# Splitting the first block's x loads over two DMA queues by partition halves

## The chip, the cores and the metric

The kernel runs on one core of a Trainium2 chip. The core has five engines that run their own instruction streams: TensorE (PE; its weight loads are shown apart as PEld), VectorE (DVE), ScalarE (ACT), GpSimd (POOL) and SyncE (SP), which only issues transfers and waits. SyncE, ScalarE and GpSimd can each issue DMA transfers on a queue of their own; the core's 16 DMA engines serve all of these queues. The metric is the time of the kernel on the device in microseconds (us); lower is better. Times are medians of several runs. A profile is one execution, with the times of every instruction and every DMA packet.

## What is computed

x is 2048 tokens of 640 features in bf16. Two branches are mixed by a gate for each token: A is linear attention with 32 heads of 20 features and a softmax feature map, B is a gated feed-forward layer of width 1728.

```python
def reference(A_x, A_wqkv, A_w_phi, A_wo, B_x, B_w_gate, B_w_up, B_w_down, gate_w):
    x = A_x
    g = _sigmoid((x * gate_w).sum(-1, keepdims=True))
    a = _A_ref(x, A_wqkv, A_w_phi, A_wo)
    b = _B_ref(x, B_w_gate, B_w_up, B_w_down)
    return g * a + (1 - g) * b

def _A_ref(x, wqkv, w_phi, wo):
    qkv = (x @ wqkv).reshape(B, S, 3, H, Dh).transpose(2, 0, 3, 1, 4)
    q, k, v = qkv[0], qkv[1], qkv[2]
    pq, pk = q @ w_phi, k @ w_phi                       # per head
    phi = lambda p: concat([softmax(p), softmax(-p)])   # for q and for k
    num = phi_q @ (phi_k.T @ v)
    den = phi_q @ phi_k.sum(0) + 1e-6
    return (num / den) @ wo

def _B_ref(x, w_gate, w_up, w_down):
    return (gelu(x @ w_gate) * (x @ w_up)) @ w_down
```

## The kernel before

The 2048 tokens are 16 tiles of 128 rows, in four blocks of four tiles. Every projection needs x with its features on the partitions (`xT`), so x must be transposed. For blocks 2 to 4 this is done by transposing DMA loads (`xturn`, L236). The first block is wanted sooner: its 512 rows are loaded as they are into `xtok` (`x4`, L227: partition p gets rows 4p to 4p+3, so the tiles are interleaved), and PE transposes them (`x_transpose`, L333). Each tile is transposed in 64-row halves, r = 0 for partitions 0 to 63 and r = 1 for 64 to 127, ten small matmuls against an identity matrix for each half. The result in PSUM is copied into `xT` by DVE (L355, tiles 0 and 2), by ACT (L353, tile 1) or by both (L350 and L351, tile 3).

`loads` (L222) gives the opening order of each queue. SyncE: the two x loads (`xload`, L229, tiles 0 and 1, then 2 and 3, 320 KB each), the v part of the attention weights in six pieces (L251, the first 128 rows in two pieces with the keys `("wv", 0)` and `"wv0"`), early up weights (L254), then transposing loads of x and of the k and q weights (L238, L234). ScalarE: an Exp on a constant (L241), ahead of which the compiler puts the load of the table of functions, then two small loads, `w_phi` (L276, which waits for a mask from GpSimd) and the gate row `gz` (L279).

`attention_state` (L684) is PE's order: nine matmuls on constants while nothing has landed (L689), the transposes of tiles 0 and 1, six small matmuls on constants (L696), the transposes of tiles 2 and 3, and then the v projection of the four tiles (`v_step`, L475, matmuls on L480). Its first steps take w piece `("wv", 0)` for tiles 0 and 1, and then `"wv0"`. After it come the gate column (L371), up projections of the first block held for later (`up_ahead`, L557), v for further tiles, and the fold of `w_phi` into the k weights (L406), which reads block-diagonal copies of `w_phi` that DVE makes (L362). The k and q projections, the Gram sums and the feed-forward layer follow, nearly all of it bound to PE.

`_Sched` sets the waits: each operation names keys that it reads and writes, and waits for the events recorded under these keys (L66). A DMA takes its queue's next lane, a semaphore of its own (L84): SyncE has 16 lanes, ScalarE 4. The keys `("xtok", t)` are read by the transposes, and by `up_ahead` (L560) and `before_num` (L857) as guards, since the memory of `xtok` is used again later.

Of the kernel before, what the change touches and what calls it, by code (L numbers as in the profile page):

```python
# [107 lines left out]
class _Kernel:  # L108
# [113 lines left out]
    def loads(self):  # L222
        sc, nc = self.sc, self.nc
# [2 lines left out]

        x4 = self.x[0:self.BT, :].rearrange("(p j) n -> p j n", j=self.TB)  # L227

        def xload(q, j):  # L229
            sc.dma(q, lambda e: e.dma_start(self.xtok[:, j:j + 2, :], x4[:, j:j + 2, :]),  # L230
                   writes=[("xtok", j), ("xtok", j + 1)])

        def wload(T, c0, key):
            sc.dma("sp", lambda e: e.dma_start_transpose(T[:, :, :], self.wqkv[:, c0:c0 + D]), writes=[key])  # L234
# [1 line left out]
        def xturn(t, n):  # L236
            a, z = t * P, (t + n) * P
            sc.dma("sp", lambda e: e.dma_start_transpose(self.xT[:, :, a:z], self.x[a:z, :]),  # L238
                   writes=[("xT", k) for k in range(t, t + n)])
        sc.op("pool", lambda e: e.memset(self.gz[:, :], 0.0), writes=["gz"])  # L240
        sc.op("act", lambda e: e.activation(self.gtmp[:, 0:1], self.nc.const_aps.tensor(1.0, [P, 1], BF16), AF.Exp),  # L241
              writes=["gtmp"])
        sc.op("pool", lambda e: e.memset(self.ident[:, :], 0.0), writes=["ident"])
        sc.op("pool", lambda e: e.affine_select(self.ident[:, :], self.ident[:, :], pattern=[[-1, P]],
                                                compare_op=ALU.not_equal, fill=1.0, base=0, channel_multiplier=1),
              writes=["ident"])
        xload("sp", 0)
        xload("sp", 2)
        for kt in range(KD):
            for a, z, key in ((0, self.VA, ("wv", 0)), (self.VA, D, "wv0")) if kt == 0 else ((0, D, ("wv", kt)),):  # L250
                sc.dma("sp", lambda e: e.dma_start(self.w3[:, kt, a:z], w3[:, kt, 2 * D + a:2 * D + z]), writes=[key])  # L251
        u3 = self.wu.rearrange("(kt p) n -> p kt n", p=P)
        a, z = self.UP[0] * P, 7 * P
# [5 lines left out]
               writes=["wul"])  # L259
# [5 lines left out]
        for i in range(KD):  # L265
# [12 lines left out]
            reads=[("mask", 1)], writes=["wphi"])  # L278
# [54 lines left out]
    def x_transpose(self, t, ek):  # L333

        sc = self.sc
        b, w = (0, 4, 2, 6)[t], self.D // 2
        bks = (b, b + 1)
        pv = self.bank(b, 1024).bitcast(BF16).rearrange("p (r c) -> p r c", r=2)[:, :, 0:w]
        for c in range(self.KD):
            for r in (0, 1):  # L340
                a = 64 * r
                sc.op("pe", lambda e: e.transpose(  # L342
                    pv[:, r, c * 64:(c + 1) * 64], self.xtok[a:a + 64, t, c * P:(c + 1) * P],
                    self.ident[a:a + 64, a:a + 64]),
                    reads=[("xtok", t), "ident"], writes=[("ps", bks[r])], signal=(c == self.KD - 1))
        out = self.xT[:, :, t * P:(t + 1) * P].rearrange("p c (r t) -> p c r t", t=64)
        src = pv.rearrange("p r (c t) -> p c r t", t=64)
        rd = [("ps", b) for b in bks]
        if ek == "ad":
            sc.op("act", lambda e: e.activation(out[:, :, 0, :], src[:, :, 0, :], AF.Copy), reads=rd[:1], writes=[("xh", t)])  # L350
            sc.op("dve", lambda e: e.tensor_copy(out[:, :, 1, :], src[:, :, 1, :]), reads=rd[1:], writes=[("xT", t)])  # L351
        elif ek == "a":
            sc.op("act", lambda e: e.activation(out, src, AF.Copy), reads=rd, writes=[("xT", t)])  # L353
        else:
            sc.op("dve", lambda e: e.tensor_copy(out, src), reads=rd, writes=[("xT", t)])  # L355
# [201 lines left out]
    def up_ahead(self, j, b, ek):  # L557
        c = (self.UP + self.LATE)[j]
        out, wk = self.upheld(c)
        old = ["wkT"] if c in self.LATE else [("xtok", k) for k in range(4)]  # L560
        for kt in range(self.KD):
            self.mm(b, 0, 512, self.wu_sb[:, kt, c * P:(c + 1) * P], self.xT[:, kt, 0:self.BT], kt == 0,
                    kt == self.KD - 1, [("xT", t) for t in range(4)] + [wk])
        if ek == "d":
            self.sc.op("dve", lambda e: e.tensor_copy(out, self.bank(b)), reads=[("ps", b)], writes=[("upf", c)],
                       guard=old)
        else:
            self.sc.op("act", lambda e: e.activation(out, self.bank(b), AF.Copy), reads=[("ps", b)], writes=[("upf", c)],
                       guard=old)
# [284 lines left out]
        return later  # L854

    def before_num(self):
        return ([("upf", c) for c in self.UP + self.LATE] + ["kstage", "qstage"] + [("wref", k, h) for k in (0, 3) for h in (0, self.HM)] + [("wref", k, 0) for k in (1, 2, 4)] + [("xtok", k) for k in range(4)] + ["wkT", "wqT"] + self.oldk)  # L857

    def num(self, t, banks=(0, 6)):
        old = self.before_num()  # L860
# [222 lines left out]
```

## Time and profile before

| | us |
|---|---|
| median of 3 runs | 281.86 |
| lowest and highest | 281.77, 281.93 |
| the profiled execution, own time | 281.68 |
| its span, first to last instruction | 280.4 |
| around the span | 1.28 |

The profile of this execution is read in views: the page with busy shares, the chain of work that ended last, the timeline of an engine, the DMA issues with their time to landing, and windows, which give busy time and DMA rate by stretch. All times in these views are microseconds from the start of the span. A line such as `4.72 0.47 PE ps L342 x20` is: start, duration, engine, what it writes, source line, count. In square brackets stands the idle time before a group and what ended it. The opening in numbers, from the DMA issues and the timelines:

| what | issued on | issue begins | to landing | first use |
|---|---|---|---|---|
| x, tiles 0 and 1, 320 KB | SyncE | 0.80 | 2.9 | 3.76 |
| x, tiles 2 and 3, 320 KB | SyncE | 1.27 | 3.4 | 4.72 |
| w `("wv", 0)`, 64 KB | SyncE | 1.73 | 3.2 | 5.12 |
| w `"wv0"`, 96 KB | SyncE | 2.19 | 3.2 | 5.43 |
| early up weights, 480 KB | SyncE | 4.57 | 4.8 | 10.66 |
| w_phi, 25 KB | ScalarE | 2.86 | 3.8 | 6.64 |

### The profile page before, as it was taken

What the parts mean: (1) busy time and instruction counts of PE and PEld (TensorE: products, weight loads), DVE (VectorE), ACT (ScalarE), POOL (GpSimd) and SP (SyncE); (2) the same over time, 40 slices, a digit from 0 to 9 for tenths busy, and PEclk for the clock granted to TensorE, in tenths of its full rate; (3) what the DMA queues carried; (4) which work ended last, traced back from release to release, by engine and by line L of the source; (5) the groups of instructions that cost most, each with busy time, mean ns of one, the idle gap of its engine ahead of it and who ended that gap; (6) DMA issues with size and microseconds to landing.
All of it is one profiled execution on the core that took longest, in us unless ns stands there. A gap on an engine that the chain in (4) does not pass through costs nothing.

```text
span 280.4 us, 7063 instructions
## 1 busy us (share of the span) xinstructions
PE 276.6 (99%) x2994; PEld 168.1 (60%) x3006; DVE 177.3 (63%) x342; ACT 106.4 (38%) x205; POOL 14.4 (5%) x69
## 2 busy tenths in 40 slices
PE   8999999999999999999999999999999999999997
PEld 4576766666765444444444444445777777777785
DVE  2666999999998524233242234878884883883801
ACT  3347877878783423222323223122112112112021
POOL 7411001101000000000000000000000000000000
DMA  7999069887899910000000000101133142232221
GB/s 217 224 220 189 6 136 165 171 163 146 162 191 273 347 41 0 2 0 0 1 2 0 0 0 2 23 2 26 26 50 108 35 76 56 62 59 66 71 75 47
DMA packets 59994, 24.11 MB, mean 86 GB/s; under 512 B 50874, under 2 KB 59450, under 8 KB 59962
## 3 DMA queue, kind: packets, MB, share of 16 engines
q1 hardware_dynamic: 59296, 23.63, 37.7%
q8 instruction: 23, 0.38, 0.6%
q10 hardware_dynamic: 666, 0.03, 0.2%
q14 instruction: 9, 0.07, 0.1%
HBM read 9.04 MB, written 2.62 MB: 42 GB/s over the span
## 4 chain that ended last, share of the span: by engine, by line
PE 97%; DMA 1%; issue 0%; SPq 0%; ACT 0%
PE ps L466 52%; PE ps L935 29%; PE ps L832 6%; PE ps L610 4%; PE ps L480 2%; PE ps L875 2%; PE ps L646 2%; DMA xtok<-in_A_x_dram 1%; PE ps L406 1%; PE ps L342 0%; SPq L230 0%; ACT outsb L948 0%; PE ps L371 0%
## 5 line engine op out<-in xcount | busy, mean ns | idle before, releaser
L809 ACT ACTIVATE gl<-ps 128x512 bf16<-128x512 f32 x52 | 31.1, 597 | 71.2 <-PE ps L466 56.3
L466 PE MATMUL ps<-xT,wu_sb 128*128 128x512 bf16 x214 | 52.9, 379 | 0.3
L466 PE MATMUL ps<-xT,wg_sb 128*128 128x512 bf16 x214 | 52.7, 379 | 0.3
L466 PE MATMUL ps<-w,xT 128*128 128x368 bf16 (+6 forms) x340 | 51.6, 303 | 0.0
L813 DVE TENSOR_TENSOR hT<-ps,gl 128x512 bf16<-128x512 f32 x34 | 23.4, 691 | 44.5 <-PE ps L466 44.5
L935 PE MATMUL ps<-wd_sb,hT 64*128 64x320 bf16 x648 | 48.2, 296 | 0.0
L948 ACT ACTIVATE outsb<-ps,Gm 128x320 bf16<-128x320 f32 (+2 forms) x31 | 14.6, 516 | 70.3 <-PE ps L935 70.3
L466 PEld LDWEIGHTS ps<-w,xT 128*128 128x128 bf16 x340 | 32.1, 98 | 14.6
L935 PEld LDWEIGHTS ps<-wd_sb,hT 64*128 64x128 bf16 x648 | 30.9, 94 | 11.8
L466 PEld LDWEIGHTS ps<-xT,wu_sb 128*128 128x128 bf16 x220 | 21.5, 98 | 25.6
L466 PEld LDWEIGHTS ps<-xT,wg_sb 128*128 128x128 bf16 x220 | 21.2, 98 | 25.2 <-issue 0.2
L935 PE MATMUL ps<-wo_sb,goT 64*128 64x320 bf16 (+2 forms) x340 | 26.5, 288 | 0.0
L628 DVE TENSOR_REDUCE Dk<-Ek 128x66 f32<-128x1320 bf16 x16 | 24.3, 1520 | 2.3 <-ACT gcol L539 2.3
L637 DVE TENSOR_TENSOR Ek<-Ek,Dk 128x1320 bf16<-128x1320 bf16 x16 | 24.5, 1533 | 0.5
L904 DVE TENSOR_TENSOR O<-ps,RH 128x640 bf16<-128x640 f32 x32 | 24.8, 815 | 0.0
L549 ACT ACTIVATE Ek<-ps 128x627 bf16<-128x627 f32 x32 | 20.5, 693 | 6.0 <-PE ps L610 4.5
L549 ACT ACTIVATE Eqt<-ps 128x627 bf16<-128x627 f32 x32 | 20.6, 704 | 2.4 <-PE ps L466 2.4
L935 PEld LDWEIGHTS ps<-wo_sb,goT 64*128 64x128 bf16 x340 | 15.8, 94 | 5.5
L832 PE MATMUL ps<-xT,wg_sb 64*128 64x512 bf16 x80 | 17.6, 376 | 0.0
L832 PE MATMUL ps<-xT,wu_sb 64*128 64x512 bf16 x80 | 17.6, 376 | 0.0
L935 PE MATMUL ps<-wd_sb,xT 64*128 64x320 bf16 (+2 forms) x270 | 16.0, 269 | 0.0
L893 DVE RECIPROCAL RH<-ps 128x32 f32<-128x32 f32 x16 | 5.7, 356 | 13.4 <-PE ps L875 13.4
(97 smaller groups left out, 222.3 us busy)
## 6 DMA issues: line engine op xcount, KB each, us to landing
out_dram<-outsb SPq DMA_DIRECT2D x7, 320.0 KB, 2.9
wd_sb<-in_B_w_down_dram SPq DMA_DIRECT2D x1, 2080.0 KB, 12.2
wg_sb<-in_B_w_gate_dram SPq DMA_DIRECT2D x5, 224.0 KB, 3.1
wg_sb<-in_B_w_gate_dram SPq DMA_DIRECT2D x5, 192.0 KB, 3.0
wu_sb<-in_B_w_up_dram SPq DMA_DIRECT2D x5, 192.0 KB, 3.9
wo_sb<-in_A_wo_dram SPq DMA_DIRECT2D x1, 800.0 KB, 10.2
xtok<-in_A_x_dram SPq DMA_DIRECT2D x2, 320.0 KB, 3.2
w<-in_A_wqkv_dram SPq DMA_DIRECT2D x4, 160.0 KB, 3.6
```

The lines of the kernel that those rows point to most:

```text
L466: self.sc.op("pe", lambda e: e.matmul(self.ps[:, bank * 512 + c0:bank * 512 + c0 + n], lhs, rhs, start=first, stop=fin), reads=reads, writ ...
L549: self.sc.op("act", lambda e: e.activation(dst, src, AF.Exp, scale=scale), reads=[("ps", b), ("ps", b + 1)], writes=[(name, sl, s)])
L610: self.sc.op("pe", lambda e: e.matmul(out, self.xT[:, kt, t * P:(t + 1) * P], self.w3[:, kt, c:c + 2 * n].rearrange("p (r w) -> p r w", w= ...
L628: self.sc.op("dve", lambda e: e.tensor_reduce(self.Dk[:, se, 0, :].rearrange("p (u h) -> p u h", h=self.HG), self.k_view(se), AX.X, ALU.ad ...
L637: sc.op("dve", lambda e: e.tensor_tensor(v, v, R.rearrange("p (u h) -> p u h", h=self.HG).unsqueeze(3).to_broadcast([P, 2 * self.G, self.H ...
L809: self.sc.op("act", lambda e: e.activation(self.gl[:, slot, :], self.bank(bank), AF.Gelu_apprx_tanh), reads=[("ps", bank)], writes=[("gl", ...
L813: self.sc.op("dve", lambda e: e.tensor_tensor(self.hT(b, c), up, self.gl[:, slot, :], ALU.mult), reads=[upk, ("gl", slot)], writes=[("hT", ...
L832: sc.op("pe", lambda e: e.matmul(self.bank(bk), w[a:a + 64, kt, c * P:(c + 1) * P], self.xT[a:a + 64, kt, b * self.BT:(b + 1) * self.BT], ...
L893: dve(lambda e: e.reciprocal(R(0), Dn[1]), rb, [key(0)], guard=old)
L904: dve(lambda e, o=o, f=f, s=s: e.tensor_tensor(o, V[s][:, :, 0:DH], f, ALU.mult), rb[2 * s:2 * s + 2] + [key(6 + s)], [("O", s, sl)], guar ...
L935: sc.op("pe", lambda e: e.matmul(self.bank(bk, w), lhs, rhs, start=opens and x == 0, stop=end and not opens, skip_group_check=True), reads ...
L948: sc.op("act", lambda e: e.activation(dst, self.bank(bk, w), AF.Copy, scale=g), reads=rd, writes=wr)
```

## The change

Each of the two x loads becomes two loads, one of partitions 0 to 63 on SyncE's queue and one of partitions 64 to 127 on ScalarE's queue. Both are placed ahead of the Exp on L241, so that ScalarE issues its two halves first. The keys get a third part, the half; a transpose of half r waits for the load of half r alone, and the later guards name both halves. Nothing else is edited: the bytes loaded and the matmuls are the same.

```diff
-        def xload(q, j):
-            sc.dma(q, lambda e: e.dma_start(self.xtok[:, j:j + 2, :], x4[:, j:j + 2, :]),
-                   writes=[("xtok", j), ("xtok", j + 1)])
+        def xload(j):
+            for q, r in (("sp", 0), ("act", 1)):
+                a = 64 * r
+                sc.dma(q, lambda e: e.dma_start(self.xtok[a:a + 64, j:j + 2, :], x4[a:a + 64, j:j + 2, :]),
+                       writes=[("xtok", j, r), ("xtok", j + 1, r)])
...
         sc.op("pool", lambda e: e.memset(self.gz[:, :], 0.0), writes=["gz"])
+        xload(0)
+        xload(2)
         sc.op("act", lambda e: e.activation(self.gtmp[:, 0:1], self.nc.const_aps.tensor(1.0, [P, 1], BF16), AF.Exp),
               writes=["gtmp"])
...
-        xload("sp", 0)
-        xload("sp", 2)
...
-                    reads=[("xtok", t), "ident"], writes=[("ps", bks[r])], signal=(c == self.KD - 1))
+                    reads=[("xtok", t, r), "ident"], writes=[("ps", bks[r])], signal=(c == self.KD - 1))
...
-        old = ["wkT"] if c in self.LATE else [("xtok", k) for k in range(4)]
+        old = ["wkT"] if c in self.LATE else [("xtok", k, r) for k in range(4) for r in (0, 1)]
```

The list in `before_num` is changed in the same way.

More of the change, by code (lines that the diff above doesn't have):

```diff
@@ L856, in before_num @@
     def before_num(self):
-        return ([("upf", c) for c in self.UP + self.LATE] + ["kstage", "qstage"] + [("wref", k, h) for k in (0, 3) for h in (0, self.HM)] + [("wref", k, 0) for k in (1, 2, 4)] + [("xtok", k) for k in range(4)] + ["wkT", "wqT"] + self.oldk)
+        return ([("upf", c) for c in self.UP + self.LATE] + ["kstage", "qstage"] + [("wref", k, h) for k in (0, 3) for h in (0, self.HM)] + [("wref", k, 0) for k in (1, 2, 4)] + [("xtok", k, r) for k in range(4) for r in (0, 1)] + ["wkT", "wqT"] + self.oldk)
     def num(self, t, banks=(0, 6)):
```

## The prediction

> **What bounds the kernel now.** I read the busy shares first: TensorE (PE) is busy in 276.6 of 280.4 us. Next the chain of waits, which says what keeps PE from its work. Its columns are start, duration (us) and what ran. Apart from the first 5 us it is PE all the way to the final output, so a shift of the point from which PE is dense goes one to one into the time.
>
> ```profile
> span 280.4 us, 7063 instructions
> PE 276.6 (99%) x2994; PEld 168.1 (60%) x3006; DVE 177.3 (63%) x342; ACT 106.4 (38%) x205; POOL 14.4 (5%) x69
> ...
> 0.80 0.40 SPq L230
> 1.21 0.06 issue
> 1.27 3.41 DMA xtok<-in_A_x_dram
> 4.68 0.05 issue
> 4.72 0.47 PE ps L342 x20
> 5.19 4.56 PE ps L480 x36
> ```
>
> So the second x load (issued at 1.27, landed 4.68) is the one on the chain. But the timeline of the weight loads (PEld) shows a second limit right behind it:
>
> ```profile
> 3.76 0.35 PEld L342 LDWEIGHTS ps<-ident,xtok 64*128 64x128 bf16 x20 [0.15 <-DMA xtok<-in_A_x_dram]
> 4.72 0.35 PEld L342 LDWEIGHTS ps<-ident,xtok 64*128 64x128 bf16 x20 [0.49 <-DMA xtok<-in_A_x_dram]
> 5.12 0.11 PEld L480 LDWEIGHTS ps<-w,xT 128*128 128x128 bf16 x2
> 5.43 2.62 PEld L480 LDWEIGHTS ps<-w,xT 128*128 128x128 bf16 x24 [0.20 <-DMA w<-in_A_wqkv_dram]
> ```
>
> The v projection does its first two steps at 5.12 and 5.24 and then waits till 5.43 for the second w piece, "wv0": 96 KB, issued on SyncE's queue at 2.19, 3.2 us to landing, so 5.39. From 5.43 PE is dense. **That 5.43 is the number to forecast.** Everything later has slack: the DMA view gives the next w piece 2.67 + 3.2 = 5.87 against a first use at 6.33, and the first up weights 4.57 + 4.8 = 9.37 against 10.66.
>
> Third, the windows of the DMA: columns are the window, busy time of each engine, clock share, DMA share and GB/s.
>
> ```profile
> 1.75:2.25 0.50, 0.50 (x3) 0.20 (x2) 0.00 (x0) 0.49 (x2) 0.39 (x3) 1.00 0.79 133
> 2.25:2.75 0.50, 0.50 (x3) 0.15 (x1) 0.00 (x0) 0.04 (x1) 0.36 (x4) 1.00 0.75 251
> 2.75:3.25 0.50, 0.50 (x2) 0.15 (x1) 0.00 (x0) 0.00 (x0) 0.36 (x4) 1.00 1.05 399
> 3.25:3.75 0.50, 0.50 (x4) 0.26 (x2) 0.00 (x0) 0.00 (x0) 0.39 (x3) 1.00 1.02 390
> ```
>
> After a ramp of 1 us, which moves 0.5 x (133 + 251) = 192 KB, the engines are full at some 395 GB/s. The two x loads are 2 x 320 KB = 655 thousand bytes, so 463 of them move in the full stretch, in 463 / 395 = 1.17 us. Bytes, not issue, set when x and the w pieces behind it land.
>
> **The change part by part.**
>
> SyncE's queue: it issues two x loads before and after, with 64 rows in place of 128. Issues take 0.40 (x, 128 rows) and 0.44 to 0.47 each for w pieces and the up weights (the six w issues span 2.80), of few or many rows alike, so I cost a half at 0.40 and leave the w issues at 1.73 and 2.19. What waits behind them on this queue (six w loads, the up weights, the transposing loads) moves by nothing. Were a half's issue cheaper, at most 0.8 would be saved there; but the w bytes would still stand behind the x bytes.
>
> ScalarE's queue, in order, from the timeline of ACT:
>
> ```profile
> 0.80 1.28 ACT L241 ACT_TABLE_LOAD   x1 [0.80 <-PEq L1068]
> 2.09 0.20 ACT L241 ACTIVATE gtmp<-const-bfloat16-1.0 128x1 f32<-128x1 bf16 x1
> 2.86 0.44 ACTq L276 DMA_DIRECT2D wphi_sb<-in_A_w_phi_dram  x1
> 3.33 0.67 ACTq L279 DMA_DIRECT2D gz<-in_gate_w_dram  x1
> 4.37 0.70 ACT L353 ACTIVATE xT<-ps 128x640 bf16<-128x640 bf16 x1 [2.07 <-PE ps L696]
> ```
>
> Two issues of 0.40 with 0.06 between go ahead: table load 1.73 to 3.01, Exp to 3.22, then the w_phi load to 3.69 (its wait for the mask ended by 2.86) and the gate row to 4.38. The copy of x tile 1 (L353) begins at 4.37 today, so ACT loses 0.01: 0.92 us of added issue lie in its idle time, 2.09 to 2.86 less the Exp, and 4.00 to 4.37. The cover is then gone: any further ACT delay puts the second projection step, which reads tile 1, behind by as much. w_phi lands some 0.4 later (6.64 to about 7.04); the block-diagonal products on DVE (L362, 2.64 us) end at 9.68 instead of 9.28, and DVE was idle for 0.56 before the gate column at 9.84; their reader on PE (L406) comes at 16.85. Nothing on the path. The gate row lands before 7.5 and is used at 9.6.
>
> Waits: each tile's transposes wait for two semaphores instead of one. Between 0 and two times the 0.05 that the chain shows at such a wait; 0, as both stand where PE waits for the later one anyway. Queued behind them on PE are the fillers and all projections.
>
> The transfers: x still has 655 thousand bytes, but as four loads of 64 rows. No x load of 64 rows is in the trace; the nearest rows are the two 80 KB loads of down weights (64 rows each), which stand in SyncE's queue between the 2080 KB load and wo's 800 KB. Counting bytes back from the end of the queue (931 thousand after 96.0, of which wo is 819), most of them move from 96.0 on:
>
> ```profile
> 95.50:96.00 0.50, 0.50 (x4) 0.24 (x3) 0.00 (x0) 0.50 (x1) 0.00 (x0) 1.00 1.22 391
> 96.00:96.50 0.50, 0.50 (x4) 0.19 (x2) 0.00 (x0) 0.03 (x1) 0.00 (x0) 1.00 1.05 256
> 96.50:97.00 0.50, 0.50 (x4) 0.24 (x3) 0.49 (x1) 0.00 (x0) 0.00 (x0) 1.00 1.01 287
> 97.00:98.00 1.00, 1.00 (x6) 0.44 (x5) 0.20 (x1) 0.41 (x1) 0.00 (x0) 1.00 1.07 339
> ```
>
> The DMA share stays at 1.0 while the rate falls from 391 to 256: the same busy engines move 64-row rows more slowly, by 391 / 256 = 1.53; over the whole dip (272 thousand bytes where 388 would go) 0.30 us is lost on 164 thousand bytes worth 0.42 us, a factor of 1.7. Bounds for x: a factor of 1.0, if a lower and an upper half under way together share what one half alone leaves unused, and 2.0, if each of the two runs at half rate. I take 1.5, the worst window of the nearest row, since here two halves are under way together. Then the second x load lands 0.5 x 1.17 = 0.59 later, at 5.27, and the w pieces behind the same bytes too: 5.39 + 0.59 = 5.98. The first x load has 328 - 192 = 136 thousand bytes in the full stretch: 0.17 later, 3.89, and ACT's copy begins at 4.54, which gives ACT back 0.16 of cover. By way of x, the projection's third step comes at 5.94; by way of w at 6.02. **Sum: 0.59 us later**, 281.68 + 0.59 = 282.27 for the profiled execution, which lies 0.18 under the median of the runs; against the median, 282.45.
>
> [...]
>
> **The rivals.**
>
> No change (N): the halves under way together fill the engines as one load did. Same bytes, same 16 engines, same issue times; x2 at 4.68, wv0 at 5.39, PE dense at 5.43: 281.86. For it: DMA share 1.05 at 395 GB/s today, so nothing to win. Against it: the dip. [...]
>
> Gain (G), the other side: two queues fill the engines faster in the ramp. From 1.75 to 2.75 they are 0.75 to 0.79 busy and move 192 where 395 would go, so at most 0.51 us is to be had, in x and w alike. It decides as long as ACT is free: L353 then cannot begin before 4.38, ends at 5.08, the second step comes at 5.12 and the third at 5.23: 0.21 sooner at most, 281.65. Beyond that, only if a half's issue costs clearly less than 0.40: with half of it ACT is free 0.4 sooner, 281.25 at best.
>
> Serial halves (S): engines all take a lower half, then all an upper half, each at half rate: factor 2, 1.17 us, 283.03. For it: both queues begin at 0.80 and keep step; the mean 1.7 of the dip. Against it: 1.53 in its worst window.
>
> The change doesn't do what it says (X): the compiler puts the table load first on ACT all the same. The ACT halves are then issued at 2.09 and 2.55; the second lands 3.4 later at 5.95, 1.27 after today's 4.68; less the 0.09 for which PE waits on w anyway, 283.04. Against it: nothing ahead of the Exp needs the table. Together with X I count a clock that falls: PE's idle time before the second transposes grows from 0.32 to some 0.8; today's 0.32 left the granted clock at 1.00.
>
> **How the numbers follow.** The forecast mechanism 0.55, its own range 282.1 to 282.8 (factors 1.2 to 1.8); N 0.17; G 0.13; S 0.10; X 0.05. 0.2% is 0.56 us, about what a measurement of this kernel can tell from no change. Of the forecast's 0.55 I put 0.33 above that line and 0.22 below; with S and X, slower 0.48. Same is 0.22 + 0.17 + 0.08 of G = 0.47; faster 0.05, the part of G with cheap issues. The range goes from G's 281.65 to S's 283.1.
>
> **What would show it.** Forecast: the DMA windows 2.75 to 3.75 under 330 GB/s at a share near 1.0; the second x load landing near 5.3; PEld's first dense L480 near 6.0. N: 4.7 and 5.4 as today. G: over 300 GB/s already before 2.75, and L353 starting at 4.38 right behind the gate row's issue. X: a table load at 0.80. I am wrong in kind if PE's dense start moves by less than 0.25, or if a later group (L406, the fold) waits where it did not.

## The result, and the profile after

| | median, us | runs | lowest to highest |
|---|---|---|---|
| before | 282.04 | 18 | 281.60 to 282.47 |
| changed | 283.66 | 18 | 282.68 to 284.85 |

The changed kernel is slower: ratio 1.0061, 95% interval 1.0046 to 1.0075, some 1.7 us. The direction was forecast, if barely (slower 0.48, same 0.47). The size was not: 0.59 us was forecast, and 283.66 lies above the range's 283.1. The 18 runs are not spread evenly. Nine lie between 282.68 and 283.05 and nine between 284.28 and 284.85, with nothing between; they are called the lower and the upper group from here on. The median of 18 runs is the mean of the two in the middle, 283.05 and 284.28, so no run took 283.66. There are two costs to explain: some 0.9 us in every execution, and another 1.7 us in half of them.

The profiled execution of the changed kernel, 282.91 us, is one of the lower nine. Its chain of waits, where L232 is the x loads, L344 the transposes and L482 the first v projection (L230, L342 and L480 before):

```profile
span 281.7 us, 7070 instructions
...
0.81 0.57 ACTq L232
1.38 0.03 issue
1.41 4.59 DMA xtok<-in_A_x_dram
6.00 0.05 issue
6.05 0.46 PE ps L344 x19
6.51 4.51 PE ps L482 x36
```

The path is the same as before, but it runs over ScalarE's queue and is 1.32 us late: the upper half of tiles 2 and 3 lands at 6.00 where the whole load landed at 4.68. The projection then takes its usual 4.51 us, and the span is 1.3 us longer. PE's weight loads show that the transposes of each pair of tiles now wait for both halves; in square brackets is the idle time and what ended it:

```profile
3.80 0.10 PEld L344 LDWEIGHTS ps<-ident,xtok 64*128 64x128 bf16 x1 [0.20 <-DMA xtok<-in_A_x_dram]
4.42 0.54 PEld L344 LDWEIGHTS ps<-ident,xtok 64*128 64x128 bf16 x19 [0.52 <-DMA xtok<-in_A_x_dram]
...
5.48 0.09 PEld L344 LDWEIGHTS ps<-ident,xtok 64*128 64x128 bf16 x1 [0.39 <-DMA xtok<-in_A_x_dram]
6.04 0.34 PEld L344 LDWEIGHTS ps<-ident,xtok 64*128 64x128 bf16 x19 [0.47 <-DMA xtok<-in_A_x_dram]
```

One transpose goes when SyncE's lower half is there, the other 19 wait 0.6 us for ScalarE's upper half, since the kernel alternates between the halves within a tile. The queues, from the timelines of SyncE and ScalarE:

```profile
0.80 1.21 SPq L232 DMA_DIRECT2D xtok<-in_A_x_dram  x2
2.05 2.95 SPq L253 DMA_DIRECT2D w<-in_A_wqkv_dram  x6
```

```profile
0.81 1.47 ACTq L232 DMA_DIRECT2D xtok<-in_A_x_dram  x2
2.31 1.28 ACT L245 ACT_TABLE_LOAD   x1 [2.31 <-issue]
2.84 0.40 ACTq L278 DMA_DIRECT2D wphi_sb<-in_A_w_phi_dram  x1
```

Two issues of halves take 1.21 us on SyncE, where two whole loads took 0.87, and 1.47 on ScalarE, 0.57 and then 0.87. The w pieces are issued 0.32 later, and `"wv0"`, at 2.68, 0.49 later; it takes 3.9 to land instead of 3.2 and is there at 6.6. The last two columns of the windows are the DMA engines' busy share and GB/s:

```profile
1.75:2.25 0.50, 0.50 (x3) 0.19 (x2) 0.00 (x0) 0.00 (x0) 0.40 (x3) 1.00 0.22 41
2.25:2.75 0.50, 0.50 (x3) 0.15 (x1) 0.00 (x0) 0.44 (x1) 0.36 (x4) 1.00 0.90 220
2.75:3.25 0.50, 0.50 (x2) 0.15 (x1) 0.00 (x0) 0.50 (x1) 0.36 (x4) 1.00 0.97 353
3.25:3.75 0.50, 0.50 (x4) 0.25 (x2) 0.00 (x0) 0.49 (x2) 0.37 (x3) 1.00 1.12 282
```

Two things are lost. The first bytes come late (41 against 133 GB/s in the first window), and later the engines are as busy as before while they move less (share 1.12 against 1.02, 282 GB/s against 390 in the last window).

### The profile page after: what moved, and what is told of

The parts are those of the page before. It is cut to its first block, busy times and chain, and to the rows that moved or that the text cites. A ratio compares the mean times of both kernels' runs of the same rounds, so it can differ in the third digit from the quotient of the medians.

```text
span 281.7 us, 7070 instructions
## 1 busy us (share of the span) xinstructions
PE 277.2 (98%) x2994; PEld 168.4 (60%) x3006; DVE 177.3 (63%) x342; ACT 106.4 (38%) x205; POOL 14.3 (5%) x69
## 4 chain that ended last, share of the span: by engine, by line
PE 97%; DMA 2%; issue 0%; ACTq 0%; ACT 0%
PE ps L468 52%; PE ps L937 29%; PE ps L834 6%; PE ps L612 4%; PE ps L482 2%; PE ps L877 2%; PE ps L648 2%; DMA xtok<-in_A_x_dram 2%; PE ps L408 1%; ACTq L232 0%; PE ps L344 0%; ACT outsb L950 0%; PE ps L373 0%
```

## The experiments

Theory R: loads of 64 rows are the cost, in their packets or in their issue. Theory Q: two queues that issue at once are the cost. Theory C: the upper group of runs is PE's clock, lost through idle time. Theory L: the upper group is loads that land later still. Each ratio below is to the kernel before on the same chip, with its 95% interval.

**Two queues, whole rows.** Against the changed kernel:

```diff
-            for q, r in (("sp", 0), ("act", 1)):
-                a = 64 * r
-                sc.dma(q, lambda e: e.dma_start(self.xtok[a:a + 64, j:j + 2, :], x4[a:a + 64, j:j + 2, :]),
-                       writes=[("xtok", j, r), ("xtok", j + 1, r)])
+            for q, t in (("sp", j), ("act", j + 1)):
+                sc.dma(q, lambda e: e.dma_start(self.xtok[:, t, :], x4[:, t, :]),
+                       writes=[("xtok", t, 0), ("xtok", t, 1)])
```

> Same four loads on the same two queues in the same places, but each of 128 rows and one tile (128 packets of 1280 B) instead of 64 rows and two tiles. Theory R (64 consecutive rows move slowly: 2560 B packets took 155 ns in the changed kernel against 102 before): the packets take 55 ns as other 1280 B packets do, the DMA rate comes back to 380 GB/s and more, the last x load lands near 5.1 instead of 6.00, PE is dense from about 5.9, median 282.3 to 282.7. Theory Q (two queues that issue at once are the cost: issues of 0.57 and 0.87 instead of 0.40, first packet of ACT's queue 0.8 later): issues as slow as in the changed kernel, last x load at 5.8 to 6.0, median 283 and more.

Measured: 282.30, ratio 1.0007 (0.9999 to 1.0016), 12 runs from 281.87 to 282.71, no upper group. Four loads on two queues with 128 rows each cost nothing that can be told from no change. The issues are as short as before, on both queues at once:

```profile
0.80 0.88 SPq L231 DMA_DIRECT2D xtok<-in_A_x_dram  x2
1.74 2.79 SPq L252 DMA_DIRECT2D w<-in_A_wqkv_dram  x6
```

```profile
0.80 0.90 ACTq L231 DMA_DIRECT2D xtok<-in_A_x_dram  x2
```

The packets of 1280 B take 55 ns in the median, as theory R had it, and the last x load lands at 4.79. Theory Q falls. What was late in the changed kernel comes from the 64 rows.

**64 rows, but every second partition.** Against the changed kernel; a tile's transposes wait for both loads:

```diff
-                a = 64 * r
-                sc.dma(q, lambda e: e.dma_start(self.xtok[a:a + 64, j:j + 2, :], x4[a:a + 64, j:j + 2, :]),
+                sc.dma(q, lambda e: e.dma_start(self.xtok[r:P:2, j:j + 2, :], x4[r:P:2, j:j + 2, :]),
...
-                    reads=[("xtok", t, r), "ident"], writes=[("ps", bks[r])], signal=(c == self.KD - 1))
+                    reads=[("xtok", t, 0), ("xtok", t, 1), "ident"], writes=[("ps", bks[r])], signal=(c == self.KD - 1))
```

> The changed kernel with one thing moved: SyncE's half is the even partitions and ScalarE's the odd ones, so each load still has 64 rows of 2560 B on its own queue, but neither is 64 consecutive partitions (each tile's transposes wait for both halves). [...] Theory Q, or theory R with the reason that 64 rows are few: packets at 150 ns, last x load at 6.0, median as the changed kernel, 283 and more.

Measured: 284.16, ratio 1.0067 (1.0045 to 1.0090); two runs at 282.8 and four from 284.1 to 284.7. As slow as the changed kernel, and yet the packets have their old pace. From the packet records, the median duration in ns of an x packet of 2560 B that begins in the stretch:

```
us                    3.0 to 3.5   3.5 to 4.0   4.0 to 4.5
before                102          102          102
changed               102          151          183
every second row      102          102          102
```

In the changed kernel ScalarE's loads write 64 partitions side by side, SyncE's the other 64, and the packets of both are slowed (median 145 and 155 ns from 3.5 to 4.0); with the partitions interleaved the median stays at 102. So it is not the count of 64 rows that slows the packets, but which 64 they are. The edit changes the rows of x that a load reads together with the partitions that it writes, and the runs do not tell these two apart. The last x load lands at 5.32 here instead of 6.00. That is still 0.64 later than before the change, and 0.68 sooner than in it. The time is not won, because the path has changed:

```profile
0.80 0.58 SPq L231
1.38 0.06 issue
1.44 0.84 SPq L231
2.27 0.05 issue
2.32 0.59 SPq L252
2.91 0.05 issue
2.96 3.54 DMA w<-in_A_wqkv_dram
6.50 0.05 issue
6.55 4.31 PE ps L481 x34
```

This is the chain of waits: three slow issues on SyncE (0.58, 0.84 and 0.59), then `"wv0"`, issued 0.77 later than before, landing at 6.50. The slow issue alone holds PE as long as the slow packets did.

**Halves on one queue.** Against the changed kernel:

```diff
-            for q, r in (("sp", 0), ("act", 1)):
+            for q, r in (("sp", 0), ("sp", 1)):
```

> The four half loads (lower and upper 64 rows) all on SyncE's queue, none on ScalarE's, which loads its table first as before. Theory R: packets of 2560 B at 140 to 160 ns though there is one queue; last x load lands at 5.3 to 5.7, and the w pieces, issued 0.93 later, behind it; PE dense from 6.3 to 6.6, median 282.8 to 283.5. Theory Q: issues at 0.40 to 0.45 each, packets at 102 ns, last x load at 4.7 to 4.9 as before, wv0 issued at 3.1 and landed at 5.9 at most, median 282.2 to 282.5.

Measured: 284.30, ratio 1.0081 (1.0064 to 1.0097), six runs from 283.19 to 285.00. The profiled run, 283.19, lies in R's range, 282.8 to 283.5, but the median lies above what either theory gave. The five runs from 284.12 on look like the upper group; none of them was profiled. In its parts R did not hold: the last half lands at 5.90 and PE is dense from 6.98, both later than R gave, and neither theory had the issues right. Four halves take 2.48 us on SyncE, 0.57 to 0.60 each, with no second queue at work. A half comes every 0.63 us, and 164 thousand bytes in that time are 260 GB/s. The packets' median stays at 102 to 113 ns, but a part of them is slower: from 2.5 to 4.5 the mean by half microsecond is 133 to 159, where the kernel before had 104 to 113. The engines' busy share is 0.94 to 0.95 from 2.75 to 4.25, at 215 to 282 GB/s. So single halves lose pace too, only less evenly.

**The issue by itself.** The kernel before, with two small loads between its x loads and the w pieces, into a buffer that nothing reads; once of 64 rows by 64 B, once of 128 rows:

```diff
         xload("sp", 2)
+        for i in (0, 1):
+            sc.dma("sp", lambda e: e.dma_start(self.scr[0:64, i, :], self.wo[0:64, 32 * i:32 * i + 32]), writes=[("scr", i)])
```

> The kernel before with two small loads of 64 rows by 64 B (4 KB each, into a buffer that nothing reads) issued on SyncE's queue between the x loads and the w pieces. Theory I (the issue of a 64-row load itself costs 0.57 to 0.60 us where a 128-row load costs 0.40 to 0.43, whatever its bytes): these issues last 0.57 to 0.60, wv0 is issued 1.25 later, at 3.45. If the issue time then goes through to the landing, wv0 lands at 6.3 to 6.7 and PE is dense 0.9 to 1.2 later, median 282.7 to 283.1, with some runs 1.7 above; if the bytes of x are what w waits for, wv0 lands by 5.7, median 282.0 to 282.3. Rival (the long issues come with the bytes of the x halves): issues of 0.40, wv0 issued at 3.1.

> The same two small loads with 128 rows by 64 B (8 KB each). Theory I: issues of 0.40 to 0.44, wv0 issued 0.9 later, at 3.1; if the issue time goes through, it lands at 5.9 to 6.3 and the median is 282.4 to 282.8; if not, by 5.6, median 281.9 to 282.2. Rival: the same issues as with 64 rows.

Measured: 64 rows 282.69, ratio 1.0020 (1.0011 to 1.0030); 128 rows 282.27, ratio 1.0008 (0.9998 to 1.0017); 10 runs each. From the chain of the first and of the second (L251 the small loads, L254 the first w piece):

```profile
1.73 0.56 SPq L251
2.28 0.04 issue
2.33 0.59 SPq L251
2.92 0.04 issue
2.96 0.59 SPq L254
```

```profile
1.72 0.42 SPq L251
2.15 0.04 issue
2.19 0.43 SPq L251
2.62 0.04 issue
2.67 0.43 SPq L254
```

The load of 4 KB in 64 rows takes longer to issue than the one of 8 KB in 128 rows, 0.56 to 0.59 against 0.42 to 0.43, and the 128-row load behind it takes 0.59 as well. So the issue goes by rows here, and not by bytes. A part of it reaches the landing: with 64 rows `"wv0"` is issued 1.40 later, at 3.59, and takes 2.7 to land, so it is there 0.88 later. The expected upper group is missing in these 20 runs, though PE is idle for 0.49 us in the first profile and 0.79 in the second between 3.5 and 6.5; why is not shown.

**Is the upper group the clock?** First, the changed kernel once more, for a profile of an execution of that group.

> The changed kernel once more, to see its loads and PE's pace side by side with the others on this chip, if it falls in the upper group. Theory C: x and w land as in the profile of the changed kernel (x at 6.0, w at 6.6), and the matmuls of the first v projection take up to twice as long till some 10 us. Theory L: x or w land at 7 and later, and the projection has its usual pace.

Measured: 284.66, 282.88, 282.72, 282.47; the profile is that of 284.66. The columns of the windows are as above, with PE's granted clock third from the end:

```profile
7.00:8.00 1.00, 1.00 (x9) 0.74 (x7) 0.94 (x5) 0.08 (x1) 1.00 (x8) 0.58 1.07 352
8.00:9.00 1.00, 1.00 (x6) 0.58 (x5) 0.88 (x5) 0.00 (x0) 1.00 (x7) 0.50 1.10 327
9.00:10.00 1.00, 1.00 (x5) 0.56 (x4) 0.79 (x4) 0.00 (x0) 0.91 (x6) 0.50 1.30 244
10.00:11.00 1.00, 1.00 (x7) 0.53 (x6) 0.00 (x0) 0.00 (x0) 0.00 (x0) 0.72 1.33 258
```

The loads land as in the lower group (the chain has the last half at 6.12, and `"wv0"` takes the same 3.9), but from 7.16 to 10.56, as the shares 0.58 and 0.72 work out, PE has half its clock: 3.40 us at half speed are 1.70 us lost. The projection shows it:

```profile
6.17 0.46 PE L344 MATMUL ps<-ident,xtok 64*128 64x64 bf16 x19 [0.76 <-DMA xtok<-in_A_x_dram]
6.56 6.22 PE L482 MATMUL ps<-w,xT 128*128 128x256 bf16 x36
```

6.22 us where the profile of the lower group has 4.57. For this execution theory L falls. Its mean granted clock reads 0.994; of the nine upper runs of the changed kernel three read 0.994 and six 1.000, so in those six a half clock is not shown. What decides which executions are hit is not shown either. The two profiles of the changed kernel differ in when PE reaches its full pace. In the upper one the 19 transposes at 4.49 take 0.46 us, as the later 19 do in both profiles, and behind them come waits of 0.08 and 0.76 us up to 6.17, after one of 0.48 ahead of them. In the lower one the 19 transposes at 4.43 still take 0.66 us, and those at 6.05 take 0.46, so full pace came later there, between two of the waits; the granted clock reads 1.00 from 4.0 to 7.0 in both. These are two executions; that this difference decides is the author's estimate, not tested.

Second, PE's waits filled. Against the changed kernel; no output needs the added matmuls:

```diff
-        for n in (512, 512, 512, 512, 512, 512, 128, 128, 128):
+        for n in (512, 512, 512, 512, 512, 512, 512, 512, 128):
...
-            for a, b in ((0, 2), (64, 3)):
-                sc.op("pe", lambda e: e.matmul(self.bank(b, P), ones[a:a + 64, 0:P], ones[a:a + 64, 0:P], start=True,
-                                               stop=True), writes=[("ps", b)])
+            sc.op("pe", lambda e: e.matmul(self.bank(b), ones[:, 0:P], ones[:, 0:512], start=True, stop=True),
+                  writes=[("ps", b)])
```

> The changed kernel with full matmuls on constants in PE's waits (two of 512 columns and one of 128 in place of three of 128 ahead of the first transposes, three of 128 rows by 512 columns in place of the six small ones; no output needs them), so PE has next to no idle time till 4.4 and about 0.4 us till 6.0. Theory C: the upper group is gone, all runs between 282.7 and 283.6, median about 283.0. Theory L: loads as in the changed kernel, the two groups stay, with runs at 284.3 and more in about half of the executions.

Measured: 282.84, ratio 1.0038 (1.0026 to 1.0050), five runs from 282.78 to 283.30. No run of the upper group is left (five runs that are hit at one in two would all escape by chance once in 32 times), and the lower one stays where it was: the loads are still late.

```profile
4.42 0.53 PE L344 MATMUL ps<-ident,xtok 64*128 64x64 bf16 x20
4.89 0.83 PE L698 MATMUL ps<-const-bfloat16-1.0 128*128 128x512 bf16 x3
5.64 0.72 PE L344 MATMUL ps<-ident,xtok 64*128 64x64 bf16 x20
```

Third, the reverse: the kernel before, loads untouched, with PE's waits emptied. All fillers of 128 columns are left out:

```diff
-        for n in (512, 512, 512, 512, 512, 512, 128, 128, 128):
+        for n in (512, 512, 512, 512, 512, 512):
...
-        for i in range(3):
+        for i in range(0):
```

> The kernel before with its loads untouched, but without the three matmuls of 128 columns ahead of the first transposes and the six small ones behind them (work on constants that no output needs), so PE is idle for about 1 us between 3.4 and 4.7 instead of 0.3. [...] Theory L (the upper group comes from loads that land later still in those executions): one group, 281.6 to 282.5 as before.

Measured: median 281.80, ratio 1.0014 (0.9996 to 1.0032), but of 12 runs nine lie from 281.61 to 282.03 and three at 283.44, 283.60 and 283.88. None of the 78 runs of the kernel before that were measured beside these kernels lies above 282.51. So leaving out PE's work brings a group some 1.9 us above, with no load touched, where theory L has one group. The profiled execution is one of the nine; no profile shows the loads of the three, and their mean granted clock reads 1.000.

A weaker filling did not do it:

```diff
-        for n in (512, 512, 512, 512, 512, 512, 128, 128, 128):
+        for n in (512, 512, 512, 512, 512, 512, 128, 128, 128, 128, 128, 128, 128, 128):
...
-        for i in range(3):
+        for i in range(14):
```

> The changed kernel with more matmuls on constants where PE waits for x: five more of 128 columns ahead of the first transposes and eleven more pairs between the second and the third (work that no output needs). [...] Without theory C: the two groups stay, runs from 282.7 to 284.8, median 283.5.

Measured: 284.17, ratio 1.0080 (1.0061 to 1.0099), six runs at 283.23, 283.76, 283.78, 284.56, 284.95 and 285.01. The two groups stayed, which speaks against theory C. The profiled execution, 283.23, has the changed kernel's span, 281.7, with 1.53 us around it where the others have 1.24 to 1.28, so all runs of this version may lie some 0.3 higher; even so three of the six are in the upper group. It differs from the full filling in that the second filler is matmuls of 64 rows by 128 columns in place of 128 by 512, and in that 14 pairs of them, which take 1.01 us from 5.01 on in this profile and end by the landing of the last half at 6.04, would by estimate take up to 2.02 us, twice that, and outlast it at half the clock. Which of the two it is was not tried; no upper run of it was profiled.

**Whole loads, one on each queue.** Against the changed kernel:

```diff
+            q = "sp" if j == 0 else "act"
+            sc.dma(q, lambda e: e.dma_start(self.xtok[:, j:j + 2, :], x4[:, j:j + 2, :]),
+                   writes=[("xtok", j + k, r) for k in (0, 1) for r in (0, 1)])
```

> Two queues with whole loads: x tiles 0 and 1 on SyncE's queue, tiles 2 and 3 on ScalarE's ahead of the table, each of 128 rows and 320 KB as before. Theory R (64-row loads are the cost, not the second queue): issues of 0.40, packets of 102 ns, the two x loads land at 3.9 to 4.6, w issued 0.47 sooner, PE dense at 5.2 to 5.5, no upper group, median 281.6 to 282.1. Theory Q (two queues at once cost): x at 5 and later, median 282.6 and more.

Measured: 282.23, ratio 1.0016 (1.0007 to 1.0024), 11 runs from 282.07 to 282.70: above R's range and below Q's, with no upper group. From its chain:

```profile
0.80 3.44 DMA xtok<-in_A_x_dram
4.25 0.05 issue
4.29 0.71 PE ps L343 x17
5.00 0.32 PE ps L697 x4
5.32 0.53 PE ps L343 x19
5.86 4.88 PE ps L481 x36
```

Side by side, the two loads share the engines and end nearly together: the first at 4.25 instead of 3.72, the second near 4.4 instead of at 4.68, with a faster ramp (179 and 369 GB/s in the first two windows against 133 and 251). `"wv0"`, issued 0.47 sooner, lands at 4.88 instead of 5.39. So the loads as a whole are sooner than before, and theory Q falls here too. What this execution, 282.67, loses against the profile before, 281.68, is PE's own pace: the chain is PE from 4.29 on, its transposes take 0.71 and 0.53 us where they took 0.47 each, and the projection 4.88 where it took 4.56, though the granted clock reads 1.00 throughout. Whether the median, 282.23, is late by the same cause is not shown. No version tried beats the kernel before.

## Why the prediction was right in direction and wrong in size

**What bounds it.** Right: the opening's delay goes one to one into the time. On the chain the first v projection begins 1.32 later, and the profiled times differ by 282.91 - 281.68 = 1.23. The number that it set out to forecast, the start from which PE is dense, came at 6.44, where it had 6.02.

**SyncE's queue: this step failed.** It read "I cost a half at 0.40 and leave the w issues at 1.73 and 2.19", argued from issues "of few or many rows alike". The loads that it went by had many packets or few, but 128 rows all the same. Two rows of its own trace spoke against it: the gate row's 0.67 for 5 rows, and the three loads of down weights, two of them of 64 rows, whose issues take 4.00 us together from 86.84 on (behind many bytes, so their cause is open). Here a half takes 0.57, ScalarE's second half 0.87, and the issue behind SyncE's halves 0.58. That puts `"wv0"` 0.49 later at its issue and the first bytes later on both queues. With every second partition, where the packets have their old pace, the issues alone kept PE till 6.55.

**The transfers.** Right in kind: 64 consecutive partitions slow the packets, and the dip at the down weights was the row to read. From 3.5 to 4.5 the packets take 151 to 183 ns against 102, a factor of 1.5 to 1.8 where 1.5 was taken. In size the term, 0.59, was near: `"wv0"` takes 0.69 longer in flight, which with 0.49 of issue makes it 1.18 later. The last x load lands 1.32 later; with every second partition it still lands 0.64 later, so by that comparison the slow packets are worth 0.68 and the issues, which the sum had at nothing, the other 0.64 (the longest issue of a half is SyncE's there, 0.84, and ScalarE's here, 0.87).

**ScalarE's queue.** The sum was made serially, and that was wrong: the w_phi load is issued at 2.84, within the table load's 2.31 to 3.59. The predicted order of things held in that ACT is not on the path; its copy of tile 1 (L355) begins at 5.20 because its input is late.

**The clock: the second step that failed.** The prediction saw PE's idle time grow and put it with rival X at 0.05, because 0.32 idle had left the clock at full. It had no term in the sum. The idle time grew to 0.98 us in the lower group's profile and to 1.32 in the upper's, in three pieces, and half of the executions lose 1.7 us; the half clock itself is shown in one of them, 284.66. Without this loss the median would be near the 282.84 of the filled kernel or the 282.89 of the lower nine, inside the range.

**The rivals.** N fell with the dip and the first windows. G was wrong in its premise: the ramp came later, not sooner. S has nearly the lower group's time, 283.03, but by another way: about 0.5 of it is issue, so its closeness is luck. X did not occur; the halves are issued at 0.81.

## What to carry to other kernels

The loads that open this kernel were best kept whole, at 128 partitions: cutting them into partition halves made each issue longer (0.56 to 0.61 us and more against 0.40) and many packets slower (151 to 183 ns against 102), and what queued behind them was late by the sum (`"wv0"` by 1.18 us). Two whole loads side by side on two queues shared the engines, so the one wanted first came later (4.25 instead of 3.72), while both together came sooner (4.4 instead of 4.68). And a wait of PE ahead of dense work is to be judged twice, for itself and for the clock: look at the spread of the runs for a second group, and try matmuls of 128 rows by 512 columns in the wait if there is one (with them none of five runs was in the upper group, without them nine of 18, and one of four on the same chip).

## What the runs showed of the hardware

- In the opening of these runs a load of 64 rows takes 0.56 to 0.61 us to issue (with two queues at work one in four takes 0.84 to 0.88), one of 128 rows 0.40 to 0.47. That holds at 4 KB against 8 KB as at 160 KB against 320 KB. The 128-row load issued next on SyncE's queue takes 0.58 to 0.59 too. Why is open.
- Loads into 64 partitions side by side, one half on each queue, slow the packets (median 102 to 151 and 183 ns); on one queue the median stays at 102 to 113 and the mean rises to 133 to 159; with every second partition on each queue the median stays at 102.
- In the one profile of the upper group PE's clock fell to half for 3.40 us, from 7.16 to 10.56 (shares 0.58, 0.50, 0.50 and 0.72 from 7.0 to 11.0), after 1.32 us of idle time in three pieces between 4.0 and 6.2, none over 0.8. In the profile of the lower group the clock reads 1.00 after 0.98 us in three pieces. That idle time is the cause is argued from the spread of the runs with PE's waits filled and emptied.
- ScalarE issues transfers while its table load runs: w_phi's at 2.84, within the table load's 2.31 to 3.59.
